# Hidden layer of the later units by sixteen block products in place of eighteen

## The chip, the core and the metric

The kernel runs on one NeuronCore of one Trainium2 chip. The metric is the device time of one execution in microseconds (us). TensorE is called PE (its weight loads PEld), VectorE DVE, ScalarE ACT, GpSimd POOL; SP is the queue that issues most transfers.

## The reference, cut to what matters

```python
# attention: B, H, S, D = 4, 8, 768, 48
f = 1.0 / (1.0 + np.exp(-f_logit))
for t in range(S):
    state = f[:, :, t, :, None] * state + np.einsum('bhd,bhe->bhde', k[:, :, t], v[:, :, t])
    y[:, :, t] = np.einsum('bhd,bhde->bhe', q[:, :, t], state)
x = y.transpose(0, 2, 1, 3).reshape(3072, 384)
# MLP: w_in 384 x 2048, w_out 2048 x 384
h = x @ w_in
g = h * (1.0 / (1.0 + np.exp(-1.702 * h)))
out = g @ w_out
```

A gated linear attention makes 3072 tokens of 384 channels, and an MLP with 2048 hidden channels follows. All is fp32. The change concerns `h = x @ w_in` and, around it, how the results leave PSUM.

## The kernel before, in words

The 3072 tokens are cut into 12 **units** of 256 (`U`), numbered 0 to 11. The attention of a unit works in six levels of a scan; its matmuls are small and wait for DVE and ACT work (`promote` multiplies the operands of the next level, L473 and L477; `set_aside` copies keys and queries, L448 and L454; `evacuate` writes the scores into `A`, L441). In between, PE works off a list called `fill`: the MLP matmuls of units whose attention is done. `merge` deals out so many columns of `fill` after each part of the attention. The order of PE is thus written by hand. Up to `fill_order.close()` all engines keep the written order; after it a scheduler orders DVE, ACT, POOL and the transfers, while PE keeps the written order.

Attention of unit n+1 overlaps the MLP of unit n. The last step of the attention of a unit (L598 on) adds the state's part to `y`, copies it to `yT` (L627) and sends it with six transfers to `xT`, which has the channels on the partitions: three blocks (`NK`) of 128 channels by 256 tokens.

The MLP of units 0 to 2 runs in blocks of four ff tiles (`mlp_block`). Units 3 to 11 run whole, by `mlp_unit`:

- `mlp_h` makes h. For each of 16 ff tiles three matmuls (one per channel block) of 128 x 128 weights against 256 tokens accumulate in one PSUM bank; ACT reads the bank once and applies the gate (`Gelu_apprx_sigmoid`, L789) into `g`. Seen as a product of blocks this is 3 ff blocks x 3 channel blocks x 2 token blocks = 18 block products, if the 16th ff tile is set aside. The four banks of tag `mm` go round.
- `sums_of_a` (L691) makes sums of quarters of g on DVE, when the quarters come.
- `mlp_o7` makes the output by seven block products where eight would be the plain way: 7 x 8 matmuls of 192 columns in four banks X, W, Y, Z, put together by ACT copies and DVE adds (`p1` to `p7`, L725 to L750) in the tile `osb`, which `store` sends out.

Unit 11 carries one more token (257 columns), since the outputs are shifted by one; that token's output is summed on DVE (`sum_last`, L797, L799) and finished by one matmul (`last_token`).

w_in and w_out arrive as 8-byte numbers and are converted on DVE and ACT during units 0 to 2 (L217 to L222); `sums_of_b` makes sums of quarters of w_out.

Tiles that the change touches: `xT` (three buffers), `g` (six buffers of four ff tiles, four for g and two for the sums `S`), `w_in` (constant, only read after the conversion), and the running scan products `tot` of `begin_gates`, which POOL makes from the gates `F` (L383).

Of the kernel before, what the change touches and what calls it, by code (L numbers as in the profile page):

```python
# [23 lines left out]
def kernel(  # L24
# [74 lines left out]

    A = const.tile([P, 2 * NP, 2, HS], F32, name="A")  # L100

    def keep_up(times, columns=384, of=None):

        if times:
            pt = ps.tile([P, columns], F32, tag="mm", name=f"idle_{next(serial)}", bufs=4)
        for _ in range(times):
            lhs, rhs = of or (ident, masks.rearrange("p l f t -> p (l f t)"))
            nc.tensor.matmul(pt, lhsT=lhs, rhs=rhs, start=True, stop=True)  # L108
# [197 lines left out]
    def attention(n):  # L306
# [19 lines left out]
        def turn(j, outs, fn=None):  # L326
# [12 lines left out]
            for j0 in range(0, R, 4):  # L339
                pt = ps.tile([P, 4, P], F32, tag="mm", name=f"t_{n}_{j}_{j0}", bufs=4)  # L340
                for jj in range(4):
# [183 lines left out]
        def turn_k(a0):  # L525
            if a0 == 0:
                new_kn()
            pt = ps.tile([P, 2, 2, P], F32, tag="mm", name=f"tkn_{n}_{a0}", bufs=4)
            for a in range(2):
                for f in range(2):  # L530
                    x = (a0 + a) * HALF
                    nc.tensor.transpose(pt[:, a, f, :], slot((KR, KF)[f])[:, x:x + HALF], ident)
            nc.scalar.copy(t["kn"][:, a0:a0 + 2], pt)
# [65 lines left out]
        def _():  # L599
# [20 lines left out]
            yT = att.tile([P, NP, NG, G], F32, tag="kn", name=f"yT_{n}", bufs=1)  # L620
            xT = xTs[n] = mlp.tile([P, NK, width(n)], F32, tag="xT", name=f"xT_{n}", bufs=3)
            for f in (1, 0):
                for g in range(NG):
# [5 lines left out]
            if n == NALL - 1:  # L629

                pl = ps.tile([P, NP], F32, tag="mm", name="y_last", bufs=4)
                for a in range(NP):
# [8 lines left out]
                yl = yl.rearrange("p (a g t) -> p a g t", g=1, t=1)  # L641
                to_x(lambda h: (yl[rows(h), :NK], lambda r, d: yl[r:r + d, NK]), xT[:, :, U:], 1)

# [46 lines left out]

    def sums_of_a(n, g, b):  # L691

        j = b % 2
        t0, t1 = slice(0, G), slice(G, 2 * G)
        tt = nc.vector.tensor_tensor
        if b < 2:
            g["S", j] = mlp.tile([P, FG, width(n)], F32, tag="g", name=f"S_{n}_{j}", bufs=6)
            tt(g["S", j][:, :, t1], g[j][:, :, t0], g[j][:, :, t1], ALU.subtract)
        else:
            tt(g[j][:, :, t1], g[j][:, :, t1], g[j + 2][:, :, t1], ALU.add)  # L700
            tt(g["S", j][:, :, t0], g[j][:, :, t1], g[j][:, :, t0], ALU.subtract)

    def last_sum(n, g):

        for j in range(2):
            by = slice(0, G)
            nc.vector.tensor_tensor(g[j + 2][:, :, by], g[j + 2][:, :, by], g["S", j][:, :, by], ALU.subtract)

    def mlp_o7(n, g):
        a = lambda i, j: lambda f: g[j * 2 + f // FG][:, f % FG, i * G:(i + 1) * G]  # L710
        s = lambda i: lambda f: g["S", f // FG][:, f % FG, i * G:(i + 1) * G]
        b = lambda i, j: lambda f: quarter(w_out, i, j)[:, f]
        T_ = lambda i: lambda f: T[i][:, f] if i < 4 else T[4](f)
        t = {}

        def out_(tt):
            if "o" not in g:
                g["o"] = mlp.tile([P, U // P, DM], F32, tag="osb", name=f"osb_{n}", bufs=1)
            return g["o"][:, tt]

        def row(name):
            t[name] = mlp.tile([P, HC], F32, tag=name, name=f"{name}_{n}", bufs=1)
            return t[name]

        def p1():  # L725
            nc.scalar.copy(row("p1"), t["X"])

        def p4():
            nc.scalar.copy(row("p4"), t["W"])

        def p2():
            nc.scalar.copy(out_(0)[:, :HC], t["X"])
            last_sum(n, g)

        def p6():
            nc.scalar.copy(row("p6"), t["Y"])

        def p5():
            nc.scalar.copy(row("p5"), t["Z"])

        def p7():
            nc.vector.tensor_tensor(row("u3"), t["p1"], t["Y"], ALU.add)
            nc.vector.tensor_tensor(out_(1)[:, :HC], t["u3"], t["p4"], ALU.subtract)
            nc.vector.tensor_tensor(out_(1)[:, HC:], t["u3"], t["p5"], ALU.add)
            store(n, 1, out_(1))

        def p3():
            nc.vector.tensor_tensor(out_(0)[:, HC:], t["p1"], t["Z"], ALU.add)
            nc.vector.tensor_tensor(out_(0)[:, HC:], out_(0)[:, HC:], t["p6"], ALU.add)
            store(n, 0, out_(0))  # L750


        products = (
            ("X", a(0, 0), b(0, 0), p1, True), ("W", a(1, 1), T_(4), p4, True), ("X", a(0, 1), b(1, 0), p2, False),
            ("Y", s(0), T_(2), p6, True), ("Z", a(1, 0), T_(1), p5, True), ("Y", s(1), T_(3), p7, False),
            ("Z", a(0, 1), b(1, 1), p3, False),
        )

        def one(bank, lhs, rhs, done, new, f):
            if new and f == 0:  # L760
                t[bank] = ps.tile([P, HC], F32, tag="mm", name=f"o_{n}_{bank}", bufs=4)
            nc.tensor.matmul(  # L762
                t[bank], lhsT=lhs(f), rhs=rhs(f), start=(new and f == 0), stop=(f == HF - 1), skip_group_check=True,
            )
            if f == HF - 1:
                done()
        return [(HC, lambda p=p, f=f: one(*p, f), 0) for p in products for f in range(HF)]


    xTs = {}  # L770

    def width(n):

        return U + (n == NALL - 1)

    def mlp_h(n, ffs, g, sums=False):
        t = {}

        def one(ff, c):
            if c == 0:  # L780
                if ff % FG == 0:
                    g[ff // FG] = mlp.tile([P, FG, width(n)], F32, tag="g", name=f"g_{n}_{ff}", bufs=6)
                t["ph"] = ps.tile([P, width(n)], F32, tag="mm", name=f"h_{n}_{ff}", bufs=4)
            ph = t["ph"]
            nc.tensor.matmul(  # L785
                ph, lhsT=w_in[:, c, ff * P:(ff + 1) * P], rhs=xTs[n][:, c, :], start=(c == 0), stop=(c == NK - 1)
            )
            if c == NK - 1:
                nc.scalar.activation(g[ff // FG][:, ff % FG, :], ph, AF.Gelu_apprx_sigmoid)  # L789
                if sums and ff % FG == FG - 1:  # L790
                    sums_of_a(n, g, ff // FG)
                if width(n) > U:

                    by = g[ff // FG][:, ff % FG, U:]
                    if ff == 0:
                        g["last"] = mlp.tile([P, 1, DM], F32, tag="sum", name="sum_last", bufs=3)
                        nc.vector.tensor_scalar(g["last"][:, 0], w_out[:, 0, :], by, None, op0=ALU.mult)  # L797
                    else:
                        nc.vector.scalar_tensor_tensor(  # L799
                            g["last"][:, 0], w_out[:, ff, :], by, g["last"][:, 0], op0=ALU.mult, op1=ALU.add  # L800
                        )
        return [(NK * U, lambda ff=ff: [one(ff, c) for c in range(NK)], ff // FG * NPC + ff % FG + 1) for ff in ffs]

    def mlp_o(n, ffs, g, done):
# [3 lines left out]
        def one(tt, ff):  # L808
            if ff == ffs[0]:
                t["po"] = ps.tile([P, DM], F32, tag="mm", name=f"o_{n}_{tt}_{ff}", bufs=4)  # L810
            nc.tensor.matmul(  # L811
# [12 lines left out]
    def mlp_unit(n):  # L824
        g = {}

        def last_token():
            po = ps.tile([P, DM], F32, tag="mm", name="o_last", bufs=4)
            nc.tensor.matmul(po[:1], lhsT=ones, rhs=g["last"][:, 0], start=True, stop=True)
# [3 lines left out]
        if width(n) > U:  # L833
            o.insert(3 * HF, (DM, last_token, 0))
        return mlp_h(n, range(NFF), g, True) + o

# [17 lines left out]

    def mlp_blocks(*blocks):

        hs, os = zip(*(mlp_block(n, r) for n, r in blocks))
        return sum(hs, []) + sum(os, [])

# [90 lines left out]

    UNIT = NFF * NK * U + U // P * NFF * DM

    load_raw(0, 0)
# [19 lines left out]
    merge(2, fill, UNIT + 3 * DM, steady, 10)  # L973
    fill += mlp_blocks((2, 0), (2, 1)) + mlp_blocks((2, 2), (0, 3)) + mlp_blocks((1, 3), (2, 3))
    merge(3, fill, 3 * UNIT // 2 - LAG // 2, steady, 7, by=0.7)
    fill_order.close()
    for n in range(3, NALL):
# [4 lines left out]
    for n in range(4, NALL):  # L982
        merge(n, fill, NFF * NK * U + 7 * HF * HC, late, chores=list(sums_of_b()) if n == 4 else ())
    for _, emit, _ in fill:
# [30 lines left out]
```

## Time and profile before

| what | value |
|---|---|
| time, median of 3 runs | 628.58 us (628.08 to 630.81) |
| profiled execution, its own time | 629.68 us |
| span of that execution, first to last instruction | 627.9 us (1.8 us lie around it) |
| PE busy | 602.8 us, 96% of the span, 7314 matmul records |
| DVE, ACT, POOL busy | 385.8 us (61%), 260.3 us (41%), 39.9 us (6%) |
| h matmuls, L785 | 257.4 us in 1152 records |
| output matmuls of units 3 to 11, L762 | four rows of the page, 52.6 + 51.9 + 24.9 + 24.9 us; a fifth row of 24.9 us is among those left out there |
| mean granted clock of TensorE | 0.989 |

How to read it: busy time of an engine is the union of its instructions, and its share of the span says how much it could matter at most. The chain of waits follows back what released what. A plain fp32 matmul leaves **two** records in the trace, each with its own weight load (L785 has 1152 records for 12 units x 16 ff tiles x 3 channel blocks = 576 matmuls); a transpose through TensorE leaves one. The mean duration of a matmul record (381 ns) holds the way through the array; what a stream of them costs is the time of a stretch divided by its records.

### The profile page before, as it was taken

The page shows a single profiled execution, that of the slowest core. Times are in us where ns is not written, and L with a number is a line of the kernel's source. Part 1 is how long each engine was busy: PE and PEld are TensorE (multiplying, and loading weights), DVE is VectorE, ACT ScalarE, POOL GpSimd, SP SyncE. Part 2 cuts the span into 40 slices and gives each one's busy share as a digit, 9 for nine tenths or more (in the row PEclk, how much of TensorE's full clock was granted, in tenths as well). Part 3 has the DMA queues.
Part 4 walks back from the last instruction along what each step waited for, and adds up shares of the span by engine and source line. Part 5 has one row for each costly group of instructions (what it writes and reads, how often), then busy time and mean ns, then how long its engine had stood idle before and what let it go on. Part 6 is the DMA issues. An engine that isn't in the chain of part 4 may idle for free.

```text
span 627.9 us, 17094 instructions
## 1 busy us (share of the span) xinstructions
PE 602.8 (96%) x7314; PEld 517.5 (82%) x7314; DVE 385.8 (61%) x632; ACT 260.3 (41%) x544; POOL 39.9 (6%) x91
## 2 busy tenths in 40 slices
PE   7958999889999999999999999999999999999997
PEld 5647776757678688989989989989989889889896
DVE  1778976575876755677566577656658645521441
ACT  3436543533244534543544454354354353233220
POOL 3010030020001001001001001001001001000000
PEclk9898999989999999999999999999999999999999
DMA  7646675652034444444452342552161121001000
GB/s 171 183 126 165 170 161 158 148 139 76 2 92 99 122 100 105 105 94 110 122 135 60 76 109 73 142 123 68 45 160 33 44 59 27 27 1 27 26 1 25
DMA packets 83308, 58.20 MB, mean 93 GB/s; under 512 B 33633, under 2 KB 75265, under 8 KB 83233
## 3 DMA queue, kind: packets, MB, share of 16 engines
q1 hardware_dynamic: 82192, 55.55, 35.4%
q10 hardware_dynamic: 1041, 1.57, 1.0%
q8 instruction: 57, 0.93, 0.7%
q14 instruction: 18, 0.15, 0.1%
HBM read 43.98 MB, written 8.39 MB: 83 GB/s over the span
## 4 chain that ended last, share of the span: by engine, by line
PE 87%; DVE 6%; ACT 3%; DMA 2%; issue 1%; SPq 1%; ACTq 0%; DVEq 0%
PE h L785 38%; PE o_X L762 8%; PE o_Y L762 8%; PE o L811 8%; PE o_Z L762 7%; PE sc L392 6%; PE o_W L762 4%; PE t L344 3%; PE y L616 2%; PE sc L576 2%; PE y L488 1%; PE idle L108 1%; DVE a L221 1%; DMA xT<-yT 1%; ACT yT L627 1%
## 5 line engine op out<-in xcount | busy, mean ns | idle before, releaser
L785 PE MATMUL h<-xT,w_in 128*128 128x256 f32 (+1 forms) x1152 | 257.4, 381 | 2.4 <-ACT g L789 1.9
L785 PEld LDWEIGHTS h<-xT,w_in 128*128 128x128 f32 x1152 | 216.4, 190 | 34.2 <-ACT g L789 2.1
L789 ACT ACTIVATE g<-h 128x256 f32<-128x256 f32 (+1 forms) x192 | 72.0, 383 | 156.8 <-PE h L785 156.5
L477 DVE TENSOR_TENSOR X<-X,tot 128x1024 f32<-128x1024 f32 x45 | 55.1, 1224 | 62.6 <-PE sc L392 49.4
L448 ACT COPY Kc<-X 128x512 f32<-128x512 f32 x72 | 48.0, 666 | 83.4 <-DVE X L477 51.3
L811 PE MATMUL o<-w_out,g 128*128 128x384 f32 x192 | 67.5, 501 | 3.0 <-DVE w_out L222 3.0
L811 PEld LDWEIGHTS o<-w_out,g 128*128 128x128 f32 x192 | 36.2, 194 | 26.0 <-DVE w_out L222 3.6
L762 PE MATMUL o_X<-w_out,g 128*128 128x192 f32 x288 | 52.6, 331 | 0.0
L762 PE MATMUL o_Y<-T,S 128*128 128x192 f32 x288 | 51.9, 329 | 0.0
L441 DVE COPY_PREDICATED A<-masks,sc 128x256 f32<-128x256 uint32 (+1 forms) x108 | 50.9, 534 | 0.1
L762 PEld LDWEIGHTS o_Y<-T,S 128*128 128x128 f32 x288 | 46.9, 190 | 1.5 <-issue 0.7
L762 PEld LDWEIGHTS o_X<-w_out,g 128*128 128x128 f32 x288 | 46.7, 190 | 1.0
L383 POOL TENSOR_TENSOR tot<-F 128x512 f32<-128x512 f32 x12 | 12.5, 1039 | 478.2 <-DVE st L594 429.3
L392 PE MATMUL sc<-X,Kc 48*64 48x64 f32 x1440 | 31.1, 224 | 10.7 <-ACT Kc L448 9.6
L392 PEld LDWEIGHTS sc<-X,Kc 48*64 48x64 f32 x1440 | 26.4, 138 | 18.0 <-ACT Kc L448 11.4
L332 DVE STREAM_TRANSPOSE X<-raw 128x512 f32<-128x512 f32 x36 | 37.9, 1101 | 2.9 <-PE y L616 2.8
L700 DVE TENSOR_TENSOR g<-g,g 128x512 f32<-128x512 f32 x18 | 12.5, 692 | 40.4 <-ACT g L789 40.4
L627 ACT COPY yT<-y 48x256 f32<-48x256 f32 x92 | 33.7, 366 | 7.8 <-PE y L616 5.3
L473 DVE TENSOR_TENSOR X<-X,tot 128x512 f32<-128x512 f32 x30 | 20.3, 688 | 13.1 <-PE sc L392 11.0
L383 POOL TENSOR_TENSOR tot<-tot 128x256 f32<-128x256 f32 (+4 forms) x60 | 24.6, 410 | 4.7
L762 PE MATMUL o_W<-T,g 128*128 128x192 f32 x144 | 24.9, 326 | 0.0
L762 PE MATMUL o_Z<-w_out,g 128*128 128x192 f32 x144 | 24.9, 326 | 0.0
(92 smaller groups left out, 629.1 us busy)
## 6 DMA issues: line engine op xcount, KB each, us to landing
bits<-in_moe_w_out_dram SPq DMA_DIRECT2D x8, 768.0 KB, 5.0
raw<-in_f_logit_dram SPq DMA_DIRECT2D x48, 96.0 KB, 2.3
raw<-in_k_dram SPq DMA_DIRECT2D x48, 96.0 KB, 2.3
raw<-in_q_dram SPq DMA_DIRECT2D x44, 96.0 KB, 2.3
bits<-in_moe_w_in_dram SPq DMA_DIRECT2D x7, 576.0 KB, 6.2
k_tok<-z SPq DMA_DIRECT2D x56, 64.0 KB, 1.8
kt<-k_tok SPq DMA_DIRECT2D x14, 256.0 KB, 2.8
out_dram<-osb SPq DMA_DIRECT2D x18, 192.0 KB, 1.8
```

The costliest lines, as they stand in the source:

```text
L332: nc.vector.transpose(view(out, at, [[HALF, NP], [step, R4], [R4 * step, 32]]), by_half[:, j, f].rearrange("p a (j d) -> p (a j) d", j=R4) ...
L383: nc.gpsimd.tensor_tensor(tn, t2[:, :, 0], t2[:, :, 1], ALU.mult)
L392: nc.tensor.matmul(t["sc"][g * HS:(g + 1) * HS, h, a, s, :], lhsT=t["Kc", l][rows(h), x:x + HS], rhs=rhs(h, a, g), start=True, stop=True,)
L441: nc.vector.copy_predicated(out=view(A, at, dims), mask=mask.bitcast(U32), data=got)
L448: nc.scalar.copy(c.rearrange("p (n two m) -> p n two m", two=2, m=m), view(X, KF * SLOT, [[2 * m, SLOT // (2 * m)], [(KR - KF) * SLOT + m, ...
L473: nc.vector.tensor_tensor(x, x, y, ALU.mult)
L477: nc.vector.tensor_tensor(x, x, y, ALU.mult)
L627: copy(view(yT[rows(h)], at, [[U, NP], [step, HS]]), py[columns(h, g), g, :, f, :])
L762: nc.tensor.matmul(t[bank], lhsT=lhs(f), rhs=rhs(f), start=(new and f == 0), stop=(f == HF - 1), skip_group_check=True,)
L785: nc.tensor.matmul(ph, lhsT=w_in[:, c, ff * P:(ff + 1) * P], rhs=xTs[n][:, c, :], start=(c == 0), stop=(c == NK - 1))
L789: nc.scalar.activation(g[ff // FG][:, ff % FG, :], ph, AF.Gelu_apprx_sigmoid)
L811: nc.tensor.matmul(t["po"], lhsT=g[ff // FG][:, ff % FG, tt * P:(tt + 1) * P], rhs=w_out[:, ff, :], start=(ff == ffs[0]), stop=(ff == ffs[ ...
```

## The change

Units 3 to 11 make 15 of the 16 ff tiles of h as a product of 3 ff blocks (of five tiles each) x 3 channel blocks x 2 token blocks, by **16** block products in place of 18. A block product takes a sum of weight blocks (`N1` to `N7`, `D..`, `C4`, or a plain block `a..`) and a sum of token blocks (`E..`, or a plain block `b..`), and 128 tokens. The 16th ff tile (`left`) is made as before.

- Each ff block is done in two groups, of three and of two tiles, so that a group's product fills at most 384 columns of one bank. The 16 products are added up in four chains; each chain runs in one bank, and at certain products the running sum of the bank is read out, while the chain goes on in the same bank afterwards. Four **lanes**, one bank each, take turns product by product (`by_step`).
- Each of six results (3 ff x 2 token blocks, per group) but one is the sum of two such readings: an ACT copy from the bank into `g`, later a DVE add of another bank onto it, then the gate on ACT, in place. The sixth is gated straight from its bank.
- `sums_of_w` makes the weight sums once: eight POOL operations and one on DVE into new tiles after `merge(3)`, and `in_place` five on POOL and three on DVE, six of the results overwriting blocks of `w_in`. `in_place` stands between the last plain h matmuls and the last plain outputs.
- `sums_of_x` makes eleven sums of token blocks (128 x 128) per unit on POOL, in two further buffers of tag `xT`.
- `g` becomes three buffers of eight ff tiles; the `mm` banks become four tags of one bank (`bank`); `mlp_o7` starts its sums in `osb`, with one DVE add fewer per unit (one instead of two after the last product Z), and takes ff tiles in the order in which they become ready; the DVE sums of g all come after `left`. The last token gets a 258th column as padding.

The diff, cut:

```diff
+    def bank(shape, name, lane=None):
+        lane = next(turns) % 4 if lane is None else lane
+        return ps.tile(shape, F32, tag=f"mm{lane}", name=name, bufs=1)
...
     def sums_of_a(n, g):
+        S = g["S"] = g_tile(f"S_{n}", width(n))
         tt = nc.vector.tensor_tensor
+        fs = [slice(f, f + HF // 2) for f in (0, HF // 2)]
+        for f in fs:
+            tt(S[:, f, t1], g[0][:, f, t0], g[0][:, f, t1], ALU.subtract)
...
         def p7():
-            nc.vector.tensor_tensor(row("u3"), t["p1"], t["Y"], ALU.add)
-            nc.vector.tensor_tensor(out_(1)[:, :HC], t["u3"], t["p4"], ALU.subtract)
-            nc.vector.tensor_tensor(out_(1)[:, HC:], t["u3"], t["p5"], ALU.add)
-            store(n, 1, out_(1))
+            plus(1, left, "Y")
+            plus(1, right, "Y")
+            store(n, 1, g["o"][:, 1])
 
         def p3():
-            nc.vector.tensor_tensor(out_(0)[:, HC:], t["p1"], t["Z"], ALU.add)
-            nc.vector.tensor_tensor(out_(0)[:, HC:], out_(0)[:, HC:], t["p6"], ALU.add)
-            store(n, 0, out_(0))
+            plus(0, right, "Z")
+            store(n, 0, g["o"][:, 0])
...
+    ROW = NFF // 3
+    GROUPS = slice(0, 3), slice(3, ROW)
+    CHAINS = (
+        (("D5", "b21", 3), ("N6", "E12", 2), ("C4", "E4", 4), ("N3", "E15", 0), ("a00", "E6", 1), ("N4", "E10", 5)),
+        (("N5", "b21", None), ("N1", "b11", 1), ("D11", "E11", None), ("D8", "E3", 0)),
+        (("a22", "E3", None), ("D9", "E9", 4), ("N7", "b10", None), ("N2", "E14", 2)),
+        (("a10", "E0", None), ("D2", "b11", 3)),
+    )
+    LANES = ((0, 0), (1, 3)), ((0, 1), (1, 1)), ((0, 2), (1, 2)), ((0, 3), (1, 0))
...
+    def sums_of_w():
...
+        both_minus("N4", "a00", "a20")
+        plus("N2", "a12", "a22")
+        plus("N6", "a20", "a21")
+        minus("N6", "N6", "N2")
+        plus("N6", "N6", "a10")
+        plus("N5", "a02", "a22")
+        plus("N5", "N5", "N4")
+        minus("N3", "a00", "a21")
+        plus("N1", "a01", "a21")
+
+        def in_place():
+            for new, old in (("D2", "a11"), ("D9", "a21"), ("D5", "a12"), ("C4", "a20"), ("D11", "a01"), ("D8", "a02")):
+                WA[new] = WA[old]
+            minus("D5", "a12", "a10")
+            plus("D2", "a10", "a11")
+            plus("D9", "a20", "a21")
+            both_minus("D11", "a01", "a00")
+            minus("C4", "a22", "a20")
+            plus("C4", "C4", "D5")
+            both_minus("D8", "D11", "a02")
+            both_minus("N7", "D2", "D9")
+        return in_place
...
+        def product(lane, group, chain, i):
...
+            for t in range(nt):
+                x = (ts.start + t) * P
+                nc.tensor.matmul(
+                    ph[:, t], lhsT=WA[a][:, x:x + P], rhs=E[n][b], start=(i == 0 and t == 0),
+                    stop=(i == len(CHAINS[chain]) - 1), skip_group_check=True,
+                )
+            if out is None:
+                return
+            to = where(group, out // 2, out % 2)
+            scale = -1.0 if out in NEGATIVE else 1.0
+            if out == CHAINS[0][-1][2]:
+                nc.scalar.activation(to, ph, AF.Gelu_apprx_sigmoid, scale=scale)
+            elif (group, out) not in begun:
+                begun.add((group, out))
+                nc.scalar.copy(to, ph)
+            else:
+                nc.vector.tensor_tensor(to, to, ph, ALU.add)
+                nc.scalar.activation(to, to, AF.Gelu_apprx_sigmoid, scale=scale)
...
-        return mlp_h(n, range(NFF), g, True) + o
+            o.insert(6 * HF, (DM, last_token, 0))
+        return mlp_h16(n, g) + o
...
-    fill += mlp_blocks((2, 0), (2, 1)) + mlp_blocks((2, 2), (0, 3)) + mlp_blocks((1, 3), (2, 3))
+    fill += mlp_blocks((2, 0), (2, 1)) + mlp_blocks((2, 2), (0, 3)) + mlp_blocks((1, 3), (2, 3), between=(lambda: in_place(),))
     merge(3, fill, 3 * UNIT // 2 - LAG // 2, steady, 7, by=0.7)
+    in_place = sums_of_w()
```

`plus` and `minus` are POOL operations, `both_minus` one on DVE (-x - y); `b` and `E` names are blocks of `xT` and sums of them.

## The prediction

> **What bounds the kernel now.** First the slices of the page:
>
> ```profile
> PE   7958999889999999999999999999999999999997
> DVE  1778976575876755677566577656658645521441
> ACT  3436543533244534543544454354354353233220
> ...
> PEclk9898999989999999999999999999999999999999
> ```
>
> From slice 11 on PE is full to the end; DVE and ACT are half idle. The longest waits of PE all lie earlier, and the windows from 160 us on show 40.0 of 40 us busy nearly throughout. So in units 3 to 11 time is what PE's stream costs, plus any wait that is put into it. The chain of waits tells the price of the stream; unit 5's h:
>
> ```profile
> 397.21 2.15 PE o_Y L762 x12
> 399.36 2.60 PE o_Z L762 x16
> 401.96 2.59 PE h L785 x12
> 405.64 18.33 PE h L785 x84
> ```
>
> An h costs 2.59 + 18.33 = 20.92 us for 96 records (0.216 to 0.218 us each, 256 columns); unit 11's 20.85. The output products cost 2.60 / 16 = 0.1625 us at 192 columns. Both fit 0.833 ns per column and 2.5 ns. Does that hold at 128 columns with 128 x 128 new weights each time? The nearest rows:
>
> ```profile
> 116.22 0.60 PE L532 MATMUL tkn<-ident,X 128*128 128x128 f32 x4
> 116.66 1.46 PE L785 MATMUL h<-xT,w_in 128*128 128x256 f32 x6
> ...
> 404.99 0.65 PE L392 MATMUL sc<-X,Kc 48*64 48x64 f32 x32
> ...
> L785 PEld LDWEIGHTS h<-xT,w_in 128*128 128x128 f32 x1152 | 216.4, 190 | 34.2 <-ACT g L789 2.1 <-issue 1.3 <-DVE sum L850 0.2
> ```
>
> Four 128-column transposes take 116.66 - 116.22 = 0.44 us, 0.110 us each, but their weight load is shorter (141 ns, by its row) than an h load (190). The scores are the closer kin: weights of 64 columns against 64 columns. A record takes (0.65 - 0.22) / 31 = 13.9 ns with four array quarters in turn, so 55.5 ns per quarter: 53.3 + 2.2, nothing lost to the load.
>
> [...] The trace's 120, 138 and 190 ns for 48, 64 and 128 columns rise by about 0.85 ns a column[...] after 2.96 us of waiting before 132.29 us the clock is 0.62 for 3.7 us and 0.92 for 4 us more, a loss of 0.38 x 3.7 + 0.08 x 4 = 1.7 us. [...] the trace has 548 for 384 (L850).
>
> **Part 1, PE's stream.** h becomes 16 products x 5 tiles = 80 matmuls, 160 records of 128 columns, plus 3 matmuls of 256 for `left`. 160 x 0.110 + 6 x 0.216 = 18.9 us for 20.92: -2.0 us. Unit 11 (129 and 258 columns): 19.0 for 20.85. Eight units and the last: **-18.0 us**. Bounds: spacing 0.109 (-19) up to 0.1625, the densest stream of such loads that the trace shows, which would be +58; each nanosecond of spacing is 1440 records, 1.44 us.
>
> **Part 2, the weight sums.** Who waits here is decided by queues:
>
> ```profile
> 197.27 1.04 POOL L383 TENSOR_TENSOR tot<-F 128x512 f32<-128x512 f32 x1 [63.60 <-DVE st L594]
> 198.39 2.09 POOL L383 TENSOR_TENSOR tot<-tot 128x256 f32<-128x256 f32 x5
> ...
> 205.44 1.22 DVE L477 TENSOR_TENSOR X<-X,tot 128x1024 f32<-128x1024 f32 x1
> ...
> 211.81 0.69 PE L392 MATMUL sc<-Qc,Kc 48*64 48x64 f32 x32
> ```
>
> In the changed program POOL does `tot` of unit 4, which can't start before 197.27, then nine sums of 640 columns up to `N1`. DVE's `D11` overwrites `a01`, which `N1` reads, and in DVE's order it stands ahead of the operand multiply of 205.44. No row shows 640 columns on POOL; 512 cost 1.04 and 256 0.69, so 1.04 + 128 x 1.35 to 1.53 ns = about 1.23 us[...]. `N1` ends at 200.5 + 9 x 1.23 = 211.6, `D9` at 212.8; DVE's three sums (0.87 each, between L799's 0.616 for 384 and L221's 1.00 for 768) end about 214.6, one transpose follows (0.95), and the multiply starts at 215.6 instead of 205.4. The scores at 211.81 need it and two ACT copies; they had some 0.7 us to spare. PE waits 10.2 - 0.7 = **+9.4 us**, once (7 if POOL takes 1.0 us[...]), and the clock then costs **+1.7** (0 to 2).
>
> **Part 3, waits inside h.** A lane goes on only when ACT or DVE has read its bank. Its turn comes after three other products: nine matmuls, 1.98 us, at first, six, 1.32 us, at the end. A reading takes 0.2 (way out of the array) + 0.48 (ACT, 384 columns, L848) or 0.55 (DVE) + 0.06: idle engines have room. But DVE comes to h with the attention's queue; from the trace before, after the scores of levels 4 and 5:
>
> ```profile
> 405.77 1.22 DVE L477 TENSOR_TENSOR X<-X,tot 128x1024 f32<-128x1024 f32 x1 [3.04 <-PE sc L392]
> 406.92 0.76 DVE L441 COPY_PREDICATED A<-masks,sc 128x256 f32<-128x256 uint32 x2
> 407.58 1.12 DVE L540 STREAM_TRANSPOSE z<-X 128x512 f32<-128x512 f32 x1
> 408.53 0.75 DVE L441 COPY_PREDICATED A<-masks,sc 128x512 f32<-128x512 uint32 x1
> ```
>
> Walk for unit 6, from the end of those scores: the multiply, copies and transpose end at 3.6 us (409.18 on that clock), two transposes at 5.5, the add for `D2` at 6.05. Lane 3 wants its bank at 5.9: wait 0.2. Further down a transpose stands ahead of the add for `a00`/`E6`, which ends at 11.4; lane 0 wants 10.9: wait 0.5. On ACT the 1.13 us copy of `kn` stands ahead of a bank copy that lane 3 needs: 0.3. With one transpose fewer ahead (units 5, 7, 9) about 0.7. Seven units (3 to 9) x 0.9, two without that queue x 0.1: **+6.4 us** (2 to 20). ACT's load in h rises from 16 x 0.383 = 6.1 to about 10 us and DVE's by 5 us; both still fit into 19.9 us beside 5 and 9 us of attention.
>
> **Part 4, the rest.** The scores of levels 2 and 3 come 4 output records (0.65 us) earlier on PE, and the sums of g, now all after `left`, push the state adds and the gates back by some 1.2 us; the chain had 1.3 us to spare. About 0.3 us in seven units: **+2** (0 to 7). The 11 token sums (128 columns on POOL, 479 ns each at most, 5.3 us) start when `xT` lands, 11 us of output products ahead of h: 0. The sums of g (6 x 0.69 us) are covered by three output products, 7.8 us: 0. `sum_last` ends about 13 us into outputs that need it after 15.6: 0. After the last product one add remains for two: **-0.4**.
>
> **Sum**: -18.0 + 9.4 + 1.7 + 6.4 + 2 - 0.4 = +1.1 us on the profiled execution's 629.68 (its span 627.9 and 1.8 around it), which stands 1.1 above the median of 628.58. On the median: 629.7, say **629.5**.
>
> **The rivals.**
>
> - **A, the gain is paid back in waits** (as summed): 40%, 623 to 636.
> - **B, the waits stay small.** POOL at 1.0 us a sum (+7, +1.2 clock), lanes always free in time (+0), +2, -0.4: -18.0 + 9.8 = -8, 620.5. For it: DVE and ACT are 30 to 50% idle here. Against: the DVE queue above, and POOL's price. 30%.
> - **C, weight loads bound the new stream.** Place: the 1440 records of 128 columns. If load and data don't overlap fully, spacing 0.120 gives +14.4 more, 644. It decides from 0.1115 on, where A's sum passes +3.1. [...] Against: the scores, at the same ratio. 13%. That the change doesn't do what it says is excluded: its PE order has the 80 matmuls.
> - **D, the queues of DVE and ACT pile up**: a late add holds a lane, PE's order holds the other lanes, and the next reading is late too. At 2.5 us a unit: 17.5 for 6.4, +12, 640.5. 17%.
>
> **How the numbers follow.** About 0.5%, 3.1 us, is what a measurement of this kernel can tell. A splits 0.35 faster, 0.37 same, 0.28 slower; B is nearly all faster; C and D slower. Faster 0.14 + 0.28 = 0.42; same 0.18; slower 0.40. The range leaves out the far tails of C and of B: 615 to 645; A's own is 623 to 636.
>
> **What would show it.** The groups: 1440 records of 128 (and 129) columns on L888, spaced 0.110. The waits of PE: one of 7 to 12 us at some 212 us, on the scores, with DVE's L809 waiting for POOL L805; then waits of L888 on DVE L902 and ACT L900 of some 7 us in all. An h with its waits of 19 to 20.5 us. Spacing over 0.115, or h over 22 us, or no wait at L809, makes the sum wrong.

## The result, and the profile after

The changed kernel takes 645.93 us (median of 4 runs, 645.10 to 647.36) against 628.85 of the kernel before beside it: ratio 1.027, 95% interval 1.024 to 1.030. **It is slower by 2.7%.** The forecast was 629.5; the value lies 0.9 us above its range of 615 to 645. The profiled execution has a span of 643.4 us, 15.5 more than the 627.9 of before.

The slices of the page after:

```profile
PE   7959999889999099999999999998999999999997
DVE  1779976566874666776767777867677765644173
ACT  3446542543145126436445545544554563343240
POOL 3010110020107910140230320311301401400200
PEclk9889999989999689999999999999999999999999
```

One slice of PE (the fourteenth, 209 to 225 us) is empty, POOL is busy just before and in it, and the clock has a 6. Elsewhere PE looks as full as before. That is deceptive, as the view of PE's waits from 200 to 600 us shows (sum, times, longest, in us):

```profile
PE sc L398 <- ACT Kc L454: 14.6, 1, 14.6
PE h L888 <- ACT g L900: 4.3, 7, 1.3
PE h L888 <- DVE g L902: 2.6, 7, 0.6
PE sc L585 <- ACT kn L564: 0.9, 2, 0.5
PE h L888 <- ACT g L897: 0.9, 2, 0.7
```

In the same stretch the kernel before has one wait:

```profile
PE sc L576 <- ACT kn L555: 0.5, 1, 0.5
```

Two things are new: one long wait, and many short ones in h.

**The stream itself** came nearly as forecast. Unit 11 has no attention beside it; the chain of waits there:

```profile
601.91 17.86 PE h L888 x160
619.77 1.31 PE h_left L908 x6
```

160 records in 17.86 us are 0.1116 us each (129 columns). In unit 6 of a later run ("the last three" below) 68 records of 128 columns without a wait took 7.59 us (378.60 to 386.19), again 0.1116. An h costs 17.86 + 1.31 = 19.17 us for 20.92.

**Inside a unit with attention** the chain looks different. Before, an h was one line of PE. After, unit 6, as the chain of waits has it:

```profile
379.71 1.13 DVE X L338
380.85 0.02 issue
380.87 0.67 ACT Qc L460
381.54 0.02 issue
381.56 1.28 ACT L903
382.84 0.01 issue
382.85 0.94 ACT g L903 x2
383.79 0.65 ACT g L900 x2
384.44 0.02 issue
384.46 0.55 DVE g L902
...
388.28 1.17 ACT kn L564
389.45 0.42 ACT g L903
389.88 0.27 ACT g L900
390.15 0.04 issue
390.19 4.30 PE h L888 x36
```

PE is not in the chain for 15 us of h (375.3 to 390.2; the view above begins inside that stretch). A bank copy (383.79) stands behind a copy of `Qc`, the load of the gelu table (the 1.28 us on L903) and two gelus; DVE's add (384.46) needs that copy; a later bank copy (389.88) stands behind `kn` and a gelu. Each of these readers frees a lane that PE's written order wants next. The table load is not new; the groups of before have it too (line, count, busy us in all, mean ns, idle before):

```profile
L789 ACT ACT_TABLE_LOAD x10 | 12.8, 1283 | 0.2
```

How much this costs is read from the timeline of PE, as the time from the first record of an h to the first output product, scores in between included. For unit 6 after:

```profile
372.65 0.83 PE L888 MATMUL h<-xT,w_in 128*128 128x128 f32 x6
...
397.68 2.54 PE L777 MATMUL o_Y<-w_out,g 128*128 128x192 f32 x14
```

For unit 7 before:

```profile
401.79 2.75 PE L785 MATMUL h<-xT,w_in 128*128 128x256 f32 x12
...
425.86 2.87 PE L762 MATMUL o_X<-w_out,g 128*128 128x192 f32 x16
```

All units, in us:

| unit | before | after | difference |
|---|---|---|---|
| 3 | 24.76 | 24.75 | -0.01 |
| 4 | 24.06 | 25.04 | +0.98 |
| 5 | 24.07 | 24.50 | +0.43 |
| 6 | 24.06 | 25.03 | +0.97 |
| 7 | 24.07 | 24.73 | +0.66 |
| 8 | 24.06 | 25.03 | +0.97 |
| 9 | 24.06 | 23.90 | -0.16 |
| 10 | 25.05 | 23.48 | -1.57 |
| 11 | 20.86 | 19.17 | -1.69 |

In unit 11, with no attention beside it, the change gains what its stream promises, and in unit 10 nearly so. With a stream shorter by 20.92 - 19.17 = 1.75 us, the rows 3 to 9 hold 1.75 + difference of waiting each: 16.1 us in all. The waits view lists only 7.8 us of it (its three rows on L888). It counts idle time from the modelled end of the record before; a record lasts 0.275 us where the next can start after 0.112, so each wait is listed some 0.16 us short, and shorter slips don't appear.

The rows add up to +0.6 us. The output stages and the tail together are 0.6 us shorter than before, so from unit 3's h on the changed kernel gains nothing and loses nothing: the waits in h take the whole gain of the stream. The 15.5 us all lie ahead of it: unit 3's h starts at 233.06 us for 217.52.

**The one wait.** POOL, DVE and PE in the timeline, in this order:

```profile
200.20 3.05 POOL L805 TENSOR_TENSOR N<-w_in 128x640 f32<-128x640 f32 x2
...
210.93 3.02 POOL L805 TENSOR_TENSOR N<-w_in 128x640 f32<-128x640 f32 x2
214.02 6.50 POOL L805 TENSOR_TENSOR w_in<-w_in 128x640 f32<-128x640 f32 x3
```

```profile
213.98 0.82 DVE L809 SCALAR_TENSOR_TENSOR w_in<-w_in 128x640 f32<-128x640 f32 x1 [10.24 <-POOL N L805]
216.22 0.82 DVE L809 SCALAR_TENSOR_TENSOR N<-w_in 128x640 f32<-128x640 f32 x1 [1.42 <-POOL w_in L805]
216.97 2.15 DVE L809 SCALAR_TENSOR_TENSOR w_in<-w_in 128x640 f32<-128x640 f32 x1
219.04 1.10 DVE L338 STREAM_TRANSPOSE X<-raw 128x512 f32<-128x512 f32 x1
219.99 1.61 DVE L483 TENSOR_TENSOR X<-X,tot 128x1024 f32<-128x1024 f32 x1
```

```profile
225.16 1.13 PE L398 MATMUL sc<-Qc,Kc 48*64 48x64 f32 x32 [14.60 <-ACT Kc L454]
226.03 1.11 PE L398 MATMUL sc<-X,Kc 48*64 48x64 f32 x32
227.07 6.15 PE L973 MATMUL o<-w_out,g 128*128 128x384 f32 x16
```

It is the predicted wait at the predicted place: `D11` on DVE waits for `N1`, the operand multiply waits behind it. A POOL sum takes 1.50 to 1.53 us. After the wait, scores and outputs up to h take 7.90 us by their starts, and the granted clock is 0.50 from 225 to 228 us. From 155 to 172 us, where the granted clock is 1.00, such scores take 1.09 us (165.22 to 166.31) and 24 output records 7.84 us (157.38 to 165.22), 0.327 each; 16 of them take 5.26 us in the run "DVE's three sums later" below (213.32 to 218.58). That makes 6.35 in all: the clock costs 1.6. The loss is not the same in each execution: in the profile of "no adds" below the wait is again 14.6 us, and the same work takes 9.41 us (225.27 to 234.68), 3.1 over the 6.35.

### The profile page after: what moved, and what is told of

The parts are those of the page before. It is cut to its first block, busy times and chain, and to the rows that moved or that the text cites. A ratio compares the mean times of both kernels' runs of the same rounds, so it can differ in the third digit from the quotient of the medians.

```text
span 643.4 us, 18718 instructions
## 1 busy us (share of the span) xinstructions
PE 596.1 (93%) x7944; PEld 529.5 (82%) x7944; DVE 427.3 (66%) x717; ACT 288.8 (45%) x598; POOL 119.4 (19%) x204
## 3 DMA queue, kind: packets, MB, share of 16 engines
q10 hardware_dynamic: 1041, 1.57, 1.0%
## 4 chain that ended last, share of the span: by engine, by line
PE 69%; DVE 11%; ACT 6%; DMA 5%; issue 3%; POOL 3%; SPq 1%; ACTq 0%; DVEq 0%; POOLq 0%
PE h L888 14%; PE o_Y L777 11%; PE o_Z L777 7%; PE o L973 7%; PE h L959 6%; PE sc L398 6%; PE o_X L777 4%; PE o_W L777 4%; DMA k_tok<-z 2%; PE t L350 2%; POOL N L805 2%; PE h_left L908 2%; DVE z L549 2%; PE y L625 2%; ACT kn L564 2%
## 5 line engine op out<-in xcount | busy, mean ns | idle before, releaser
L888 PE MATMUL h<-E,w_in 128*128 128x128 f32 (+1 forms) x630 | 86.7, 277 | 2.6 <-DVE g L902 1.7
L888 PEld LDWEIGHTS h<-E,w_in 128*128 128x128 f32 x630 | 77.6, 192 | 4.2 <-DVE g L902 2.3
L902 DVE TENSOR_TENSOR g<-g,h 128x384 f32<-128x384 f32 (+3 forms) x90 | 42.9, 487 | 47.8 <-PE h L888 36.4
L959 PE MATMUL h<-xT,w_in 128*128 128x256 f32 x288 | 66.5, 384 | 2.4 <-ACT g L963 1.9
L959 PEld LDWEIGHTS h<-xT,w_in 128*128 128x128 f32 x288 | 53.5, 190 | 11.8 <-ACT g L963 2.1
L900 ACT COPY g<-h 128x256 f32<-128x256 f32 (+3 forms) x90 | 37.9, 426 | 55.8 <-PE h L888 55.8
L888 PE MATMUL h<-E,N 128*128 128x128 f32 (+1 forms) x360 | 51.2, 279 | 5.5 <-ACT g L900 4.3
L903 ACT ACTIVATE g<-g 128x384 f32<-128x384 f32 (+3 forms) x90 | 41.1, 470 | 27.2 <-DVE g L902 26.6
L888 PEld LDWEIGHTS h<-E,N 128*128 128x128 f32 x360 | 44.8, 192 | 8.3 <-ACT g L900 6.5
L888 PE MATMUL h<-xT,N 128*128 128x128 f32 (+1 forms) x270 | 39.1, 275 | 0.0
```

Source lines behind the costliest of these rows:

```text
L888: nc.tensor.matmul(ph[:, t], lhsT=WA[a][:, x:x + P], rhs=E[n][b], start=(i == 0 and t == 0), stop=(i == len(CHAINS[chain]) - 1), skip_grou ...
L900: nc.scalar.copy(to, ph)
L902: nc.vector.tensor_tensor(to, to, ph, ALU.add)
L903: nc.scalar.activation(to, to, AF.Gelu_apprx_sigmoid, scale=scale)
L959: nc.tensor.matmul(ph, lhsT=w_in[:, c, ff * P:(ff + 1) * P], rhs=xTs[n][:, c, :], start=(c == 0), stop=(c == NK - 1))
```

## The experiments

Each run is the changed kernel with the edit shown; ... marks what is left out of it. Ratios are to the kernel before, run beside it.

**Early sums.** Where does the one wait go if POOL makes its sums while it is idle?

```diff
-            lambda: ve.tensor_tensor(dst, a, s, ALU.add),
+            lambda: (ve.tensor_tensor(dst, a, s, ALU.add), m == LAST_IN and early.append(sums_of_w())),
...
-    in_place = sums_of_w()
+    in_place, = early
```

> The sums of weights that need storage of their own (N1 to N6, 10 of the 16 instructions) are made as soon as the last column pair of w_in is converted, at some 161 us, where POOL is idle, and not behind POOL's products of unit 4's gates. Theory (one wait bought by the queues of POOL and DVE): D11 on DVE no longer waits for N1; the wait of 14.6 us of PE on scores at 211 us goes to 0 to 4 us, with the slow clock after it (2 us), while the waits inside h stay: 646 - 12 to 16 = 630 to 634 us. Rival 1 (the scores were late for another reason, say operands or raw loads): the wait keeps over 10 us, 641 to 646. Rival 2 (the sums only take their wait along, to DVE's conversions of w_out that share the time with POOL): the wait at 211 us goes, but conversion and the fill blocks end later by about as much, 638 to 646.

Measured: 643.48 us, ratio 1.023 (1.020 to 1.025), as rival 2 had it. The wait at 211 us is down to 0.6 us, but another has come. PE's waits from 150 us on have

```profile
PE h L960 <- DVE sum L1013: 10.9, 1, 10.9
...
PE sc L400 <- ACT Kc L456: 0.6, 1, 0.6
```

and DVE's timeline tells why (lines are shifted by two):

```profile
163.43 1.89 DVE L227 TENSOR_SCALAR s<-a 128x768 int32<-128x768 int32 x1
165.24 2.29 DVE L694 TENSOR_TENSOR T<-w_out 128x768 f32<-128x768 f32 x1
...
175.37 4.21 DVE L810 SCALAR_TENSOR_TENSOR w_in<-w_in 128x640 f32<-128x640 f32 x2 [5.57 <-POOL N L806]
```

The scheduler moved `D11` forward with the sums, so DVE again waits for POOL at the head of its queue (5.57 us), and beside POOL DVE's conversions and sums are longer: 1.89 for 0.55 (L227), 2.29 for 0.95 (L694), both by 1.34 us. The addition is the same for these two instructions and a little under one POOL sum (1.50); what holds them up was not shown. Elsewhere it is smaller: two operand multiplies beside POOL take 2.24 and 2.46 for 1.23 us in the next run. Transposes beside POOL keep their 1.1 us there (1.08 to 1.11).

**DVE's three sums later, alone.** `evacuate` calls them for the last level of unit 4; the product of one column makes them wait for `A`.

```diff
+                if n == N_FILL + 1 and m == 32:
+                    last["sums"](A[:, 0, 0])
...
-            both_minus("D11", "a01", "a00")
...
-            both_minus("D8", "D11", "a02")
-            both_minus("N7", "D2", "D9")
...
+        def on_dve(e):
+            nc.vector.tensor_tensor(WA["N7"][:, :1], e[:, :1], WA["a01"][:, :1], ALU.mult)
+            both_minus("D11", "a01", "a00")
+            both_minus("N7", "D2", "D9")
+            both_minus("D8", "D11", "a02")
...
```

> One edit alone: DVE's D11, N7 and D8 come after the scores of levels 4 and 5 of unit 4, in the first microseconds of unit 3's h, by a reading of A that they have to wait for; POOL's order and all else are those of the changed kernel. Theory (the 14.6 us were D11 waiting for N1 at the head of DVE's queue): the wait on scores at 211 us is gone, and POOL is what is late next: D5, D2, D9, C4 and the token sums of unit 3 follow N1 at 214 us and end at some 228 to 230 us for an h that could start at 217.5; so 6 to 11 us of waiting come back on h's products of N or E tiles, 635 to 641. Rival (the wait at 211 us was the contention of POOL and DVE, not the order): a wait of over 8 us on scores stays, 643 to 647.

Measured: 640.03 us, ratio 1.017 (1.015 to 1.019). The theory holds, and POOL is indeed next: in PE's waits from 195 to 260 us

```profile
PE h L893 <- POOL E L851: 5.9, 2, 4.5
PE sc L398 <- ACT Kc L456: 1.0, 1, 1.0
```

So the order of DVE's queue made the 14.6 us. The time fell by only 5.9 us, since unit 3's h, which starts earlier, now waits 5.9 us for POOL's token sums, and PE is slow again behind that wait: 18 records of h take 3.93 us by their starts (228.68 to 232.61), 0.218 us each for 0.1116.

**Sixteen products from unit 4 on, sums spread.** `mlp_h18` is h with eighteen products, as before; `in_place` comes after the first two output products of unit 3, and its products of one column hold `D5`, `D2` and `D9` back until unit 5's gates are made. DVE's three sums are delayed as in the run before, by one unit more.

```diff
-            if n >= N_FILL:
+            if n > N_FILL:
                 sums_of_x(n)
...
+        if n == N_FILL:
+            o.insert(2 * HF, (0, lambda: in_place(), 0))
+            return mlp_h18(n, g) + o
...
+            for x in ("a12", "a11", "a21"):
+                nc.gpsimd.tensor_tensor(after, last["tot"][:, 1007:1008], WA[x][:, :1], ALU.mult)
...
+                if n == N_FILL + 2 and m == 32:
+                    last["sums"](A[:, 0, 0])
```

> Unit 3 keeps the eighteen products (plain h of 256 columns); the sixteen begin with unit 4, and the sums of weights are spread: N1 to N6 on POOL behind unit 4's gates, as before, but nothing on DVE waits for them; D5, D2, D9 and C4 on POOL among unit 3's output products; D11, N7 and D8 on DVE in the first microseconds of unit 4's h. Theory (the one wait came from D11 ahead of the operand multiply in DVE's queue, plus contention when all 18 sums are done within 30 us): no wait over 2 us at 211 us, unit 4's h starts 14 to 16 us earlier than in the changed kernel (264 to 266 us), at most 3 us of new waits in unit 4's h: 629 to 634 us. Rival (POOL's sums slow DVE so much, wherever they stand, that the chain of the scores is late anyway): waits of over 5 us on scores or state scores between 197 and 245 us, 636 to 645.

Measured: 628.72 us, ratio 1.000 (0.9985 to 1.0011), a little better than the theory's 629 to 634. From 195 us on the longest wait on scores is 0.6 us; unit 4's h starts at 262.21 us for 279.58. The one wait, its clock and unit 3's h, together 17.2 us of the time, were a matter of when the sums are made and first needed.

**The waits inside h.** Four runs take out three suspects one by one, the table load in two ways, and a fifth run all three together. First, the gelu table loaded early, by a gelu of one column after the sigmoid of F:

```diff
+                    if n > N_FILL:
+                        early_gelu = att.tile([P, 1], F32, tag="eg", name=f"eg_{n}", bufs=1)
+                        nc.scalar.activation(early_gelu, F[:, :1], AF.Gelu_apprx_sigmoid)
```

> After the sigmoid of F in units 4 to 11 ACT does a gelu of one column, so that the table of gelu is loaded among the output products and no longer in the middle of h, between a copy of Qc and the gelus and bank copies that are queued behind it. Theory (the waits inside h come from ACT's queue, in which the 1.28 us table load and 0.7 us Qc stand ahead of the copies that free the lanes): h to the first output product falls from 24.5 - 25.0 us to about 23.5 to 24.0 in units 4 to 8, total -3 to -7 us: 639 to 643. Rival (DVE's queue alone sets the adds): h stays at 24.5 to 25.0, 645 to 647. Rival 2 (the matmul stream itself is slower in h beside other work): no change either, and the small gaps between records stay where they are.

The same after the first bank copy of h, in `product`:

```diff
+                nc.scalar.copy(to, ph)
+                if not begun:
+                    early = att.tile([P, 1], F32, tag="eg", name=f"eg_{n}", bufs=1)
+                    nc.scalar.activation(early, to[:, 0, :1], AF.Gelu_apprx_sigmoid)
                 begun.add((group, out))
-                nc.scalar.copy(to, ph)
```

> As in the run before with an early gelu, but the one-column gelu follows the first bank copy of h, where ACT has 3.5 us of nothing to do. Theory: the gain in h of units 4, 6 and 8 stays (24.0 to 24.1 for 25.0 us), and the waits on scores of 1.0 us, which the table load put into the output products, are gone (unit to unit 45.8 to 46.5): 641 to 644. Rival (the gain came from elsewhere, since later readings were moved by the wait): 645 to 647.

`kn` copied by POOL:

```diff
-            nc.scalar.copy(t["kn"][:, :, f, :], z.rearrange("p d a -> p a d"))
+            nc.gpsimd.tensor_copy(t["kn"][:, :, f, :], z.rearrange("p d a -> p a d"))
```

> The copy of kn (two of 1.14 us in each of units 4 to 10) goes from ACT to POOL. Theory (ACT's queue holds lanes): the wait of 0.3 to 0.5 us on a bank copy behind kn in the last third of h goes; h falls by 0.3 to 0.6 us in units 4 to 9, total -2 to -4 us, 642 to 644, unless POOL's copy (some 1 to 2 us each, with the gates' products and token sums) makes the state scores late after h, which would show as a wait of L585 of 1 us or more. Rival (DVE's queue alone): 645 to 647 or slower.

No adds on DVE; this kernel leaves out one of the two banks of each block of h, and shows only what the adds cost in time:

```diff
-                nc.vector.tensor_tensor(to, to, ph, ALU.add)
-                nc.scalar.activation(to, to, AF.Gelu_apprx_sigmoid, scale=scale)
+                nc.scalar.activation(to, ph, AF.Gelu_apprx_sigmoid, scale=scale)
```

> The ten adds of DVE in h of each unit are left out: the gelu reads the second bank alone, so one of the two banks that make up a block of h is missing from the output. ACT has the same number of instructions, PE the same stream. Theory (lanes are held by readers in the queues of DVE and ACT, DVE's adds being the later ones): waits inside h fall from some 2.8 us to below 1 us per unit, h to the first output product 22.5 to 23.2 us in units 3 to 9, total -10 to -15 us, 631 to 636. Rival (ACT alone: table load, Qc, kn): waits stay above 2 us, 641 to 646. Rival 2 (stream itself): no change at all.

The last three edits together (this kernel too leaves out one bank):

> The changed kernel with DVE's ten adds of h left out (one of the two banks of each block of h is missing from the output), kn on POOL and the table load in the gap; the sums of weights stay as they are. Theory (the waits inside h are nothing but late readings by DVE and ACT): h to the first output product 22.1 to 22.6 us in units 4 to 8, the stream (19.0) plus the 3.1 us of scores and state scores that the kernel before has there too. Rival (the lanes' own latency, or 128-column records beside scores, costs 0.5 us or more per unit): 22.8 us or more. The time: 646 - 13 to 16 = 630 to 633, the wait at 212 us being still there.

Measured, h to the first output product, units 4 to 9:

| run | 4 | 5 | 6 | 7 | 8 | 9 | time, ratio (interval) |
|---|---|---|---|---|---|---|---|
| changed kernel | 25.04 | 24.50 | 25.03 | 24.73 | 25.03 | 23.90 | 645.93, 1.027 (1.024 to 1.030) |
| early gelu | 24.07 | 24.47 | 24.00 | 24.75 | 24.03 | 23.90 | 651.49, 1.036 (1.033 to 1.039) |
| table in the gap | 23.94 | 24.43 | 23.96 | 24.70 | 23.98 | 23.86 | 641.99, 1.022 (1.019 to 1.025) |
| kn on POOL | 24.62 | 23.50 | 24.63 | 23.86 | 24.64 | 22.70 | 642.74, 1.021 (1.018 to 1.025) |
| no adds | 23.03 | 23.24 | 22.81 | 23.42 | 22.81 | 23.40 | 635.55, 1.010 (1.008 to 1.012) |
| the last three | 23.50 | 22.64 | 22.84 | 22.64 | 22.84 | 23.13 | 633.03, 1.006 (1.004 to 1.008) |

The kernels of this table keep the one wait, and behind it a loss of 1.6 to 3.1 us from one execution to the next; so they are compared by these stages, and the times beside them only in the rough.

- The table load costs 1.1 us in each of units 4, 6 and 8 and nothing in 5 and 7. The early gelu shortened h in 4, 6 and 8 as expected and was yet 5.6 us slower: right behind the sigmoid's load it put the gelu's, ahead of ACT's copies for the scores. PE's waits from 232 to 520 us then begin with `PE sc L401 <- ACT Kc L457: 6.9, 6, 1.5`, which the changed kernel has not. In ACT's idle time after the first bank copy the same load is free.
- The copy of `kn` costs 0.4 us in units 4, 6, 8, and 0.9 to 1.2 in 5, 7, 9. After the move the wait on ACT's bank copies falls from 4.3 to 0.6 us.
- DVE's adds cost 1.3 to 2.2 us (0.5 in unit 9). Without them, and with as many ACT instructions as before, the waits on L888 that the view lists fall from 7.8 to 1.3 us.
- With all three gone units 5 to 8 stand at 22.64 to 22.84, that is 1.2 to 1.4 below before, of 1.75 possible. That is just above the theory's 22.1 to 22.6, and 22.84 touches the rival's 22.8; unit 4 stays at 23.50 and unit 9 at 23.13. Late readers are thus most of the waiting but not shown to be all of it. ACT's copy of `Qc`, a fourth suspect in the chain of unit 6, still stands among the bank copies in this run; what the last 0.3 to 0.5 us are was not tried.
- The parts overlap: in units 5 to 9 table, kn and adds alone gain 2.3 + 3.9 + 7.5 = 13.7 us, together 9.1. An add that is late because ACT's copy is late counts in both.

**The rest of the change, alone.** Eighteen products everywhere (`return mlp_h18(n, g) + o`), no sums of weights or tokens; the rest of the change stays.

> The changed kernel with the eighteen products of 256 columns in every unit, so without sums of weights and of tokens; the rest stays (output rows added up in place, sums of g all after h, four banks by name, scores of levels 2 and 3 a little earlier, one add fewer at the end). Theory (the rest of the change is neutral on this machine, as the output stages of 21.9 us in both profiles say): 627.5 to 629.5. Rival (the prediction's part 4: the chain of the state is pushed back by 0.3 us per unit): 630 to 633.

Measured: 629.36 us, ratio 1.000 (0.998 to 1.001), as the theory had it. The rest is neutral.

**Putting it together.** The edits of "sixteen products from unit 4 on", "table in the gap" and "kn on POOL" in one kernel:

> Three edits together: sixteen products from unit 4 on with the spread sums, the table of gelu loaded in the gap after the first bank copy of h, and kn copied by POOL. Theory (queue effects that add up): 646 less 14 to 16 (stall), 3 to 4 (table), 3 to 4 (kn) = 622 to 627, below the kernel before (629). Rival (the waits are on the same lanes, and what one edit frees the next reader takes, so that the gains overlap): 627 to 632.

Measured: 624.04 us, ratio 0.993 (0.991 to 0.995), faster than the kernel before by 0.7% and inside the theory's 622 to 627. The ACT part of unit 6 now reads

```profile
357.83 0.48 ACT L908 COPY g<-h 128x384 f32<-128x384 f32 x1 [1.38 <-PE h L897]
358.32 1.28 ACT L911 ACT_TABLE_LOAD   x1
359.62 0.20 ACT L911 ACTIVATE eg<-g 128x1 f32<-128x1 f32 x1
361.79 0.48 ACT L908 COPY g<-h 128x384 f32<-128x384 f32 x1 [1.97 <-PE h L897]
```

with 2 us of idle time left after the load. In units 5 to 9 h is 6.2 us shorter than in the changed kernel, the sum of table (2.3) and kn (3.9): these two add up. The same stages for this kernel and two further steps from it:

| run | 4 | 5 | 6 | 7 | 8 | 9 |
|---|---|---|---|---|---|---|
| the three edits | 25.24 | 23.48 | 23.54 | 23.82 | 23.58 | 22.60 |
| the three and Qc on POOL | 25.09 | 24.28 | 23.64 | 24.31 | 23.63 | 24.09 |
| the three and late gelus | 24.94 | 23.31 | 23.61 | 23.80 | 23.57 | 22.58 |

The first step, `Qc` of level 0 copied by POOL:

```diff
-                nc.scalar.copy(
+                (nc.gpsimd.tensor_copy if l == 0 and n > N_FILL else nc.scalar.copy)(
                     c.rearrange("p f (n m) -> p f n m", m=m),
```

> The three edits together, and ACT's copy of Qc of level 0 (0.67 us, in h) goes to POOL. Theory (ACT's queue still holds a reader by up to its length): another 0 to 0.3 us in units 5 to 9, 622 to 624. Rival (only DVE's adds are left as late readers): 624 as before, or 1 to 3 us more if POOL's copy is later than ACT's and the multiply of level 0 behind it on DVE pushes adds back.

Measured: 626.92 us, ratio 0.996 (0.995 to 0.997), 2.9 us worse than the three edits, as the rival had it. POOL's copy of `kn` now follows that of `Qc` and lies beside the multiply of level 0, which stands ahead of adds in DVE's queue and takes longer:

```profile
328.92 1.13 POOL L567 COPY kn<-kt 128x512 f32<-128x512 f32 x1
```

```profile
329.17 1.96 DVE L486 TENSOR_TENSOR X<-X,F 128x1024 f32<-128x1024 f32 x1 [0.61 <-ACT Kc L457]
```

1.96 us for 1.23 with the three edits. Units 5, 7 and 9 lose 0.5 to 1.5 us.

The second step, instead of that, gelus four products later:

```diff
-                nc.scalar.activation(to, to, AF.Gelu_apprx_sigmoid, scale=scale)
+                waiting.append([4, lambda: nc.scalar.activation(to, to, AF.Gelu_apprx_sigmoid, scale=scale)])
...
```

> The three edits together, and the ten gelus of h that work from SBUF to SBUF (they free no bank) are issued four products later, so that the copies that do free banks come ahead of them in ACT's queue. Theory (any instruction ahead of a bank reader in its queue costs its length, as far as the lane has no slack): another 0.2 to 0.5 us in units 4 to 9, 621 to 623. Rival (what is left are DVE's adds behind transposes, and a gelu that is late at the end of h delays the sums of g): 624 to 626.

Measured: 622.86 us, ratio 0.990 (0.988 to 0.992), the shortest time of all; but units 4 to 9 differ from the three edits by +0.07 to -0.30 us, 0.45 less in all, which is under the spread of either kernel's executions (1.8 and 2.7 us). That the later gelus gain is thus not shown.

## Why the prediction was wrong, point by point

On the profiled executions the sum was +1.1 us; measured is +15.5. The miss of 14.4 is made of +2.3 (part 1), +5.1 (part 2), +9.9 (part 3), -2 (part 4) and -0.9 outside the parts.

- **Part 1**, -18.0: measured -15.7 (eight units of 1.75 and 1.69 in the last). Spacing 0.1116 for 0.110, over 1440 records 2.3 us. It was read from four transposes with a shorter load (141 ns for 192). Rival C was to decide from 0.1115 on; the spacing is just there, and far from the 0.120 by which C was priced. So new weights for each 128 columns cost next to nothing here: the fit of the prediction (0.833 ns a column and 2.5 ns) gives 0.109.
- **Part 2**, +9.4 and +1.7 for the clock: measured 14.6 and 1.6. Mechanism and place were right, the sizes not. POOL's sum was taken as 1.23 us from the slope between 256 and 512 columns; it was 1.50 to 1.53, and `N1` ended 213.95 for 211.6. From there to the multiply 4.0 us were expected and 6.0 measured: the in-place sums were priced one by one, but POOL and DVE do them at the same time and slow each other (2.15 for 0.82 on DVE, 2.18 for 1.5 on POOL, 214.02 to 216.20 in the chain). That the clock cost came out as forecast is luck in part, since the loss was 3.1 us behind the same wait in another execution.
- **Part 3**, +6.4: measured 16.1 in units 3 to 9 and 0.2 in unit 10. **This is the step that failed most.** It walked through DVE's queue and found 0.5 here and 0.2 there, priced `kn` at 0.3 where its removal gained 0.4 to 1.2, and left out the table load, 1283 ns each time. With eighteen products three other banks of six records, 1.3 us each, gave ACT some 3.9 us of room for it; a lane of the sixteen has room of 1.3 to 2 us, and there the load cost 1.1 us in each of units 4, 6 and 8. The walk also took each lateness as used up once, while a late copy makes an add late, and the add another lane: the overlap of the parts (13.7 alone, 9.1 together) and the chain of unit 6 speak for that. This was rival D, which got 17% and a price of 2.5 us per unit: measured 2.3 (16.1 over 7). The lines that the prediction shows for units 5 and 6 (397 to 410 us of before) are unit 7's, whose h starts at 401.79; in unit 6 DVE's four lines take as long (359.94 to 363.43), so no term changes by it.
- **Part 4**, +2: not there. From the first output product to the next h it is 21.8 us in both kernels, and the run with the rest of the change alone is level with before. The tail's -0.4 came as forecast (22.9 to 22.5 us from the last unit's first output product to the end).

Measured terms: -15.7 + 16.2 + 16.3 - 0.4 = 16.4; of the 0.9 that this is above 15.5, 0.7 lie ahead of unit 3's h.

Of four things that were to show it right, two came true: the records, and listed waits of "some 7 us" (7.8). The wait of DVE on POOL came in its place, but longer than 7 to 12 us, the author's estimate. The fourth, h with its waits at 19 to 20.5 us, did not come: 20.92 + 0.97 = 21.9 in unit 6. None of the three signs that were to make the sum wrong came either (0.1116 is not over 0.115, 21.9 not over 22, and the wait at L809 is there), so they were set too wide for a sum that was 14.4 us off. The listed waits were the weaker test.

## What to carry over

When a change shortens what lies between two uses of a buffer, walk the queues of its readers again with everything in them that takes longer than the new slack, table loads included: what 3.9 us of room hid is exposed by room of 1.3 to 2 us. Preparatory work on an idle engine is not free if an instruction that waits for it stands at the head of another engine's queue (14.6 us here), and POOL's sums and DVE's sums, at the same time, slow each other (2.15 us for 0.82 on DVE, 2.18 for 1.5 on POOL). Judge a stage by its whole duration, since a view of waits leaves the small ones out.

## What was not expected of the hardware

- A POOL sum of 640 fp32 columns takes 1.50 to 1.53 us alone, and up to 2.42 beside DVE's work in the run with DVE's sums later. On DVE, beside POOL, 0.82 became 2.15, 0.55 became 1.89 and 0.95 became 2.29, each 1.33 to 1.34 more; a multiply of 1.23 became up to 2.46.
- A load of 128 x 128 fp32 weights stays nearly hidden under 128 columns of data in a long stream: 0.1116 us a record, with loads that last 192 ns in the trace.
- A load of ACT's table takes 1.283 us in each group of the profiles before and after; a gelu of one column (0.20 us) is enough to choose the place.
- Behind the same wait of PE, 14.6 us, 64 score records and 16 output records took 7.90 us in one profile, with a granted clock of 0.50 from 225 to 228 us, and 9.41 in another, for 6.35.
